# Splitting one group of products into 192 and 320 tokens, and issuing two row halves in order of time

## Chip, cores, metric

One core of a Trainium2 chip runs the kernel. The metric is the device time of one execution in microseconds (us); the time stated for a kernel is the median over its runs.

## The reference

The input x is 4 x 4096 x 192 (16384 tokens of 192 channels). A causal convolution of 7 taps with softmax weights per head goes ahead of two feed-forward blocks of 192 -> 2048 -> 192:

```python
x   = conv(x, softmax(weight))          # (16384, 192)
h1  = x @ moe_w_in                      # (16384, 2048)
x   = maximum(h1, 0) ** 2 @ moe_w_out   # (16384, 192)
h2  = x @ moe2_w_in
out = where(h2 > 0, h2, exp(minimum(h2, 0)) - 1) @ moe2_w_out
```

## The kernel before

The tokens go in 32 blocks of TB = 512. For each block and layer the 2048 hidden channels go in NP = 8 chunks of 256; one chunk of one block of one layer is a unit, and there are NU = 512 units. A planner (`merge` and `phases`) lists the units once; the main loop takes them in that order. In the round of unit u the kernel computes the first product h of unit u (`gemm1`), and the second product of unit u - 3 (`gemm2`, LAG = 3).

Every fp32 operand is kept as an upper part and a lower part in the type fp32r, and a product is the sum of three: upper by upper, upper by lower, lower by upper. After `gemm1`, ScalarE and VectorE make g from h, and split it into `gh` and `gl` (lines 740 and 745). `gemm2` multiplies g with the weights `wo`: its part A makes output channels 0 to 127 in the PSUM tile yA, with six products for a unit (four with `gh`, two with `gl`), its part B the last 64 channels in yB, with four products of which two are with `gl` (mostly 96 weight columns wide). `gemm1` makes two tiles h[0] and h[1] of 128 hidden channels, with nine products for each and row half, as listed below.

The contraction is cut across the TensorE's rows: each product is issued as two, one with rows 0 to 63 and one with rows 64 to 127. They are called half 0 and half 1, and each has its own list. All of them are 64 rows, 128 (or 96) weight columns and 512 tokens, and each loads its own weights (LDWEIGHTS, engine PEld in the profile). `products` (line 519 issues them) walks both lists in four turns, given by TURNS:

- turn 0: half 0 does part A (6), half 1 does part B (4)
- turn 1: half 0 does its work for h[0] (6), half 1 for h[1] (6)
- turn 2: half 0 does part B (4), half 1 does part A (6)
- turn 3: half 0 does h[1] (3), half 1 does h[0] (3)

So each half has 19 products in a unit. Before the change they are issued in pairs by `zip`: product k of half 0, then product k of half 1. So that the halves never add to the same PSUM tile at once, some products wait for the end of the other half's work on that tile: a `nop` on SyncE (line 524) waits for the product with index 5, 11 or 15 of half 1, and product 10 of half 1, 16 of half 0 or 0 of half 0 (of the next unit) waits for that nop. The same SyncE queue also issues most of the DMAs.

This form runs for u >= HALVES = 16 while both products exist, that is in rounds 16 to 511, 496 of them. Rounds 0 to 15 and the last three use lines 532 and 538: line 532 issues products over all 128 rows, and line 538 pairs of 64 rows for the first product's B rows. The convolution of the first blocks is done on TensorE in plain fp32 (line 400).

Of the kernel before, what the change touches and what calls it, by code (L numbers as in the profile page):

```python
# [19 lines left out]
TB = 512  # L20
# [45 lines left out]
def conv_moe_moe_kernel(  # L66
# [17 lines left out]
    nc = tc.nc  # L84
    B, S, D = x.shape
# [5 lines left out]
    DB = D - P  # L91
# [74 lines left out]
    def w_tiles(layer):  # L166
        if layer not in WS:
            tag = "w" if layer == 2 else "w1"
            WS[layer] = {
                s: cpool.tile([P, *dims], F32R, tag=f"{tag}{s}", name=f"w{s}{layer}") for s, dims in W_PARTS.items()  # L170
            }
        return WS[layer]
# [308 lines left out]
    def gemm2(layer, j, i, gh, gl):  # L481

        if i == 0:
            Y[layer, j] = [ps_y.tile([P, TB], F32, tag="y", name=f"y{layer}{s}") for s in "AB"]
        o = w_tiles(layer)["o"]
        hi, lo, b, bl = slice(0, P), slice(D + DB, 2 * D), slice(P, D + DB), slice(P, D + DB // 2)
        todo = {
            "A": [(s, d, g) for s in range(2) for d, g in ((hi, gh), (lo, gh))] + [(s, hi, gl) for s in range(2)],
            "B": [(s, b, gh) for s in range(2)] + [(0, bl, gl), (1, bl if i < NP - 1 else b, gl)],
        }  # L490
        work = {}
        for half in range(2):
            for y, part in zip(Y[layer, j], "AB"):
                begins = i == 0 and half == "AB".index(part)
                ends = i == NP - 1 and half != "AB".index(part)
                last = len(todo[part]) - 1
                work[half, part] = [
                    (o[:, 2 * i + s, d], g[:, s, :], y[0 : d.stop - d.start], begins and k == 0, ends and k == last)
                    for k, (s, d, g) in enumerate(todo[part])
                ]  # L500
        return work

# [1 line left out]


    TURNS = (("A", 0, "B", 1), ("B", 1, "A", 0))
    SIGNALS, WAITS = (5, 11, 15), {(10, 1): 5, (16, 0): 11, (0, 0): 15}
    SYNC = mybir.DependencyInfo(mybir.DependencyClass.Sync, mybir.DependencyReason.DATA)
    signals = {}

    def products(first, second, halves):

        if first and second and halves:
            work = {**first, **second}
            todo = [[w for what in TURNS[half] for w in work[half, what]] for half in range(2)]
            for k, pair in enumerate(zip(*todo)):
                for half, (w, x, o, st, sp) in enumerate(pair):
                    p = slice(half * DB, (half + 1) * DB)
                    m = nc.tensor.matmul(o, w[p], x[p], start=st, stop=sp)  # L519
                    after = signals.pop(WAITS.get((k, half)), None)  # L520
                    if after:
                        tc.add_manual_dep(m.ins, after.ins.name, SYNC, reason="the other half's products")
                    if half and k in SIGNALS:
                        signals[k] = nc.sync.nop()  # L524
                        tc.add_manual_dep(signals[k].ins, m.ins.name, SYNC, reason="the halves' products")
            return
        for do, parts in ((first, (0, 1)), (second, ("A", "B"))):
            for part in parts if do else ():
                order = (0, 1) if part in (0, "A") else (1, 0)
                begins, ends = (do[half, part] for half in order)  # L530
                for (w, x, o, st, _), (_, _, _, _, sp) in zip(begins, ends):
                    nc.tensor.matmul(o, w, x, start=st, stop=sp and part in ("A", "B"))  # L532
            if do is first and first:
                for k in range(3, 6):
                    for half in range(2):
                        w, x, o, _, _ = first[half, half][k]
                        p = slice(half * DB, (half + 1) * DB)
                        nc.tensor.matmul(o, w[p], x[p], start=False, stop=k == 5)  # L538
# [162 lines left out]
    with tc.manual_schedule():  # L701
# [61 lines left out]
        for u in range(NU + LAG):  # L763
# [12 lines left out]
            if 0 <= v:  # L776
                second = gemm2(*units[v], *gsplit.pop(v))
            products(u < NU and first, 0 <= v and second, u >= HALVES)
            for _ in range(3 if u < FIRST * NP else 2):
                if transfers and transfers[0][0] <= u:  # L780
# [65 lines left out]
```

## Time and profile before

| | |
|---|---|
| median of the runs | 2318.26 us (2318.13 to 2318.39) |
| the profiled execution's own time | 2319.63 us |
| its span, first to last instruction | 2317.9 us |
| granted TensorE clock, mean | 0.998 |
| busy: PE, PEld, DVE, ACT, POOL | 99%, 93%, 71%, 68%, 3% |
| matmul instructions, weight loads | 19282 each |

PE is TensorE's matmuls, PEld its weight loads, DVE VectorE, ACT ScalarE, POOL GpSimd, SPq the queue of SyncE. A matmul's record lasts longer than the distance to the next one, since matmuls are pipelined and their ends modelled; what one costs is read from the distance between the starts of two neighbours of the same half. The busy shares are averages over the span.

### The profile page before, as it was taken

The numbers are of one execution on the slowest core, as the hardware profiler recorded it, in microseconds if no ns is written. First come the engines' busy times: TensorE is split into PE (matmuls) and PEld (weight loads), VectorE is DVE, ScalarE is ACT, GpSimd is POOL, SyncE is SP. The second block draws the span as 40 slices with busy tenths as digits, with TensorE's granted clock in tenths as the row PEclk, the third lists the DMA queues.
The fourth block names the chain that finished last, engine by engine and source line by source line (L and its number), as shares of the span: only waits on it lengthen the run. The fifth ranks groups of instructions, "written<-read, shape, count | busy, mean of one in ns | idle before, by whom it ended". The sixth has DMA issues, their size and how long they took to land.

```text
span 2317.9 us, 46408 instructions
## 1 busy us (share of the span) xinstructions
PE 2305.2 (99%) x19282; PEld 2161.3 (93%) x19282; DVE 1652.1 (71%) x1968; ACT 1570.1 (68%) x1726; POOL 64.6 (3%) x81
## 2 busy tenths in 40 slices
PE   8999999999999999999999999999999999999999
PEld 5788998899999999999999999999999999999998
DVE  7768676777777776777767777777777676666665
ACT  7788888666666666666666666666666666777776
POOL 0012221000000000000000000000000000000000
PEclk9999999999999999999999999999999999999999
DMA  5112111111111111111111111111111110111111
GB/s 143 28 44 47 43 47 28 31 31 28 31 19 33 33 29 31 22 28 35 30 29 31 20 33 33 28 31 20 30 35 31 26 26 19 33 22 28 31 22 19
DMA packets 236721, 75.88 MB, mean 33 GB/s; under 512 B 208608, under 2 KB 220384, under 8 KB 236512
## 3 DMA queue, kind: packets, MB, share of 16 engines
q1 hardware_dynamic: 235440, 72.79, 14.2%
q8 instruction: 152, 2.49, 0.5%
q14 instruction: 57, 0.47, 0.1%
q10 hardware_dynamic: 1072, 0.13, 0.0%
HBM read 41.94 MB, written 25.17 MB: 29 GB/s over the span
## 4 chain that ended last, share of the span: by engine, by line
PE 97%; ACT 1%; DVE 1%; issue 0%; POOL 0%; SPq 0%; DVEq 0%; POOLq 0%; ACTq 0%
PE h L519 44%; PE y2A L519 15%; PE y1A L519 15%; PE y2B L519 10%; PE y1B L519 9%; PE h L532 1%; PE y1A L532 1%; PE h L538 1%; PE conv L400 1%; PE y1B L532 0%; ACT r L542 0%; ACT r L551 0%; PE warm L389 0%; PE y2A L532 0%; ACT gh L740 0%
## 5 line engine op out<-in xcount | busy, mean ns | idle before, releaser
L745 DVE TENSOR_TENSOR gl<-r,gh 128x1024 fp32r<-128x1024 f32 x512 | 633.7, 1238 | 410.4 <-ACT gh L740 410.4
L740 ACT CAST gh<-r 128x1024 fp32r<-128x1024 f32 x512 | 537.6, 1050 | 502.0 <-DVE r L555 292.3
L542 ACT ACTIVATE r<-h 128x1024 f32<-128x1024 f32 x512 | 525.1, 1026 | 193.7 <-PE h L519 184.4
L519 PE MATMUL y2A<-gh,wo 64*128 64x512 f32 x2024 | 554.1, 393 | 0.0
L519 PE MATMUL y1A<-gh,wo 64*128 64x512 f32 x1944 | 530.4, 392 | 0.7 <-SPq L524 0.6
L555 DVE SCALAR_TENSOR_TENSOR r<-r,h 128x1024 f32<-128x1024 f32 x256 | 312.7, 1222 | 205.7 <-ACT r L546 205.1
L519 PEld LDWEIGHTS y2A<-gh,wo 64*128 64x128 f32 x2024 | 356.2, 185 | 2.4
L519 PEld LDWEIGHTS y1A<-gh,wo 64*128 64x128 f32 x1944 | 345.2, 184 | 9.2 <-SPq L524 1.9
L519 PE MATMUL h<-x2Al,wAh 64*128 64x512 f32 x1024 | 323.5, 393 | 0.0
L519 PE MATMUL h<-x2Ah,wAl 64*128 64x512 f32 x1024 | 321.8, 391 | 0.0
L519 PE MATMUL h<-x2Ah,wAh 64*128 64x512 f32 x1024 | 321.4, 391 | 0.0
L519 PE MATMUL y2A<-gl,wo 64*128 64x512 f32 x1012 | 318.9, 395 | 0.0
L519 PE MATMUL y2B<-gh,wo 64*128 64x512 f32 x1012 | 316.3, 392 | 0.0
L519 PE MATMUL y2B<-gl,wo 64*96 64x512 f32 x1012 | 316.0, 392 | 0.0
L519 PE MATMUL y1A<-gl,wo 64*128 64x512 f32 x972 | 303.2, 391 | 0.0
L519 PE MATMUL y1B<-gh,wo 64*128 64x512 f32 x972 | 303.2, 391 | 0.0
L519 PE MATMUL y1B<-gl,wo 64*96 64x512 f32 x972 | 302.1, 390 | 0.0
L519 PE MATMUL h<-x1Ah,wAh 64*128 64x512 f32 x960 | 301.2, 393 | 0.0
L519 PE MATMUL h<-x1Ah,wAl 64*128 64x512 f32 x960 | 299.8, 391 | 0.0
L519 PE MATMUL h<-x1Al,wAh 64*128 64x512 f32 x960 | 299.6, 391 | 0.0
L546 ACT ACTIVATE r<-r 128x1024 f32<-128x1024 f32 x256 | 271.5, 1061 | 8.1
L553 DVE SCALAR_TENSOR_TENSOR r<-h,r 128x1024 f32<-128x1024 f32 x176 | 215.3, 1223 | 25.0 <-ACT r L542 22.9
(158 smaller groups left out, 4685.3 us busy)
## 6 DMA issues: line engine op xcount, KB each, us to landing
kept<-ya SPq DMA_DIRECT2D x32, 256.0 KB, 2.4
la<-kept SPq DMA_DIRECT2D x32, 256.0 KB, 3.1
lb<-kept SPq DMA_DIRECT2D x64, 128.0 KB, 3.0
out_dram<-zA SPq DMA_DIRECT2D x128, 64.0 KB, 2.0
xinA<-in_x_dram SPq DMA_DIRECT2D x126, 64.0 KB, 2.3
xinB<-in_x_dram SPq DMA_DIRECT2D x128, 32.0 KB, 1.9
kept<-ys SPq DMA_DIRECT2D x32, 128.0 KB, 2.4
out_dram<-zB SPq DMA_DIRECT2D x64, 64.0 KB, 2.0
```

What stands on the lines that cost most here:

```text
L400: nc.tensor.matmul(st[i], diag(i, k), t[:, k : k + n], start=k == 0, stop=k == K - 1)
L519: m = nc.tensor.matmul(o, w[p], x[p], start=st, stop=sp)
L532: nc.tensor.matmul(o, w, x, start=st, stop=sp and part in ("A", "B"))
L538: nc.tensor.matmul(o, w[p], x[p], start=False, stop=k == 5)
L542: nc.scalar.activation(out=r, in_=h, func=AF.Relu, scale=1.0 if layer == 1 else -1.0)
L546: nc.scalar.activation(out=r, in_=r, func=AF.Exp, scale=-1.0)
L553: nc.vector.scalar_tensor_tensor(out=r, in0=h, scalar=0.0, in1=r, op0=ALU.max, op1=ALU.mult)
L555: nc.vector.scalar_tensor_tensor(out=r, in0=r, scalar=-1.0, in1=h, op0=ALU.add, op1=ALU.max)
L740: nc.scalar.copy(out=gh, in_=gs[u])
L745: nc.vector.tensor_tensor(out=gl, in0=gs.pop(u), in1=f32(gsplit[u][0]), op=ALU.subtract)
```

## The change

In `gemm2`, each of part A's products with `gl` becomes two: one over tokens 0 to 191 and one over tokens 192 to 511, with the same weights and the same columns of yA. Each half has two such products in a unit, so its list grows from 19 products to 21. In `products`, the pairs of `zip` give way to a choice by time: each half has a clock that grows by the tokens of a product plus LOAD = 48, and the half whose clock is behind (half 0 at a tie) issues next. The nops and waits are placed by turns in place of indices: after both halves' last product of turns 0, 1 and 2 comes a nop, and the first product of turn 2, turn 3 and the next unit's turn 0 waits for it.

```diff
@@ -483,6 +483,7 @@
         o = w_tiles(layer)["o"]
+        WHOLE, CUT = (slice(0, TB),), (slice(0, D), slice(D, TB))
         hi, lo, b, bl = slice(0, P), slice(D + DB, 2 * D), slice(P, D + DB), slice(P, D + DB // 2)
@@ -495,8 +496,9 @@
                 work[half, part] = [
-                    (o[:, 2 * i + s, d], g[:, s, :], y[0 : d.stop - d.start], begins and k == 0, ends and k == last)
+                    (o[:, 2 * i + s, d], g[:, s, t], y[0 : d.stop - d.start, t], begins and k == 0, ends and k == last and t.stop == TB)
                     for k, (s, d, g) in enumerate(todo[part])
+                    for t in (CUT if g is gl and part == "A" else WHOLE)
                 ]
@@ -504,7 +506,7 @@
     TURNS = (("A", 0, "B", 1), ("B", 1, "A", 0))
-    SIGNALS, WAITS = (5, 11, 15), {(10, 1): 5, (16, 0): 11, (0, 0): 15}
+    LOAD = 48
@@ -512,17 +514,24 @@
             work = {**first, **second}
-            todo = [[w for what in TURNS[half] for w in work[half, what]] for half in range(2)]
-            for k, pair in enumerate(zip(*todo)):
-                for half, (w, x, o, st, sp) in enumerate(pair):
-                    p = slice(half * DB, (half + 1) * DB)
-                    m = nc.tensor.matmul(o, w[p], x[p], start=st, stop=sp)
-                    after = signals.pop(WAITS.get((k, half)), None)
+            todo = [deque((n, w) for n, what in enumerate(TURNS[half]) for w in work[half, what]) for half in range(2)]
+            clock, begun, last = [0, 0], set(), {}
+            while todo[0] or todo[1]:
+                half = 0 if todo[0] and (not todo[1] or clock[0] <= clock[1]) else 1
+                n, (w, x, o, st, sp) = todo[half].popleft()
+                p = slice(half * DB, (half + 1) * DB)
+                m = nc.tensor.matmul(o, w[p], x[p], start=st, stop=sp)
+                clock[half] += x.shape[-1] + LOAD
+                if n not in begun:
+                    begun.add(n)
+                    after = signals.pop((n + 2) % 4, None) if n != 1 else None
                     if after:
                         tc.add_manual_dep(m.ins, after.ins.name, SYNC, reason="the other half's products")
-                    if half and k in SIGNALS:
-                        signals[k] = nc.sync.nop()
-                        tc.add_manual_dep(signals[k].ins, m.ins.name, SYNC, reason="the halves' products")
+                last[n, half] = m
+                if n < 3 and (n, 1 - half) in last and all(not t or t[0][0] > n for t in todo):
+                    signals[n] = nc.sync.nop()
+                    for k in range(2):
+                        tc.add_manual_dep(signals[n].ins, last[n, k].ins.name, SYNC, reason="the halves' products")
             return
```

## Rows read from the trace of the kernel before

**Rows 1.** The page's part 1: busy time of each engine, share, instructions.

```profile
PE 2305.2 (99%) x19282; PEld 2161.3 (93%) x19282; DVE 1652.1 (71%) x1968; ACT 1570.1 (68%) x1726; POOL 64.6 (3%) x81
```

**Rows 2.** The page's part 4: the chain that ended last, by engine.

```profile
PE 97%; ACT 1%; DVE 1%; issue 0%; POOL 0%; SPq 0%; DVEq 0%; POOLq 0%; ACTq 0%
```

**Rows 3.** Busy time by stretch (instructions in brackets), granted clock, DMA share, GB/s.

```profile
105.30:2303.90 2198.60, 2197.89 (x18843) 2088.83 (x18843) 1563.37 (x1805) 1486.10 (x1597) 60.92 (x66) 1.00 0.14 30
```

**Rows 4.** Groups of instructions by form, PE: count, busy us, mean ns.

```profile
L519 PE MATMUL y2A<-gl,wo 64*128 64x512 f32 x1012 | 318.9, 395 | 0.0
...
L519 PE MATMUL y1A<-gl,wo 64*128 64x512 f32 x972 | 303.2, 391 | 0.0
```

**Rows 5.** Timeline, PE: the same turn of two units; start us, length us.

```profile
1201.57 0.58 PE L519 MATMUL h<-x2Ah,wAh 64*128 64x512 f32 x2
...
1206.01 0.59 PE L519 MATMUL h<-x1Ah,wAh 64*128 64x512 f32 x2
```

**Rows 6.** Timeline, part of turn 2: matmuls and weight loads, half 0 y2B, half 1 y2A.

```profile
1202.97 0.39 PE L519 MATMUL y2A<-gh,wo 64*128 64x512 f32 x1
1202.97 0.18 PEld L519 LDWEIGHTS y2A<-gh,wo 64*128 64x128 f32 x1
1203.16 0.40 PE L519 MATMUL y2B<-gh,wo 64*128 64x512 f32 x1
1203.17 0.18 PEld L519 LDWEIGHTS y2B<-gh,wo 64*128 64x128 f32 x1
1203.21 0.40 PE L519 MATMUL y2A<-gh,wo 64*128 64x512 f32 x1
1203.21 0.18 PEld L519 LDWEIGHTS y2A<-gh,wo 64*128 64x128 f32 x1
...
1203.40 0.39 PE L519 MATMUL y2B<-gh,wo 64*128 64x512 f32 x1
...
1203.67 0.39 PE L519 MATMUL y2A<-gh,wo 64*128 64x512 f32 x1
```

**Rows 7.** One line's instructions, L519 weight loads: min/median/max ns.

```profile
L519 PEld LDWEIGHTS y2B<-gh,wo x1012: 183/185/188, 402.9 to 2303.0; 64*128 64x128 f32 x169
...
L519 PEld LDWEIGHTS y2B<-gl,wo x1012: 157/158/188, 403.3 to 2303.4; 64*96 64x96 f32 x169
```

**Rows 8.** One line's instructions, L538: first product after the full-row products, and second.

```profile
L538 PE MATMUL h<-x1Bh,wBh x32: 493/498/792, 21.4 to 101.9; 64*128 64x512 f32 x32
...
L538 PE MATMUL h<-x1Bh,wBl x32: 388/389/628, 21.7 to 102.2; 64*128 64x512 f32 x32
```

**Rows 9.** Timeline of that place: L532's last product, then L538's pairs.

```profile
82.28 0.40 PE L532 MATMUL h<-x1Al,wAh 128*128 128x512 f32 x1
82.61 0.19 PEld L538 LDWEIGHTS h<-x1Bh,wBh 64*128 64x128 f32 x2 [0.37 <-issue]
82.61 0.51 PE L538 MATMUL h<-x1Bh,wBh 64*128 64x512 f32 x2
...
82.71 0.19 PEld L538 LDWEIGHTS h<-x1Bh,wBl 64*128 64x128 f32 x2
82.94 0.40 PE L538 MATMUL h<-x1Bh,wBl 64*128 64x512 f32 x2
```

**Rows 10.** One line's instructions, L400, the fp32 convolution: two matmuls a tap.

```profile
L400 PE MATMUL conv<-xtB,x2Bl x12: 378/378/379, 11.4 to 25.2; 128*128 128x256 f32 x12
...
L400 PE MATMUL conv<-xtA,x2Al x12: 591/592/697, 16.1 to 36.0; 128*128 128x512 f32 x12
```

**Rows 11.** Timeline, PE: five of the convolution's matmuls of 256 tokens.

```profile
24.11 1.24 PE L400 MATMUL conv<-xtB,x2Bl 128*128 128x256 f32 x5
```

**Rows 12.** Timeline, PE, L532's products over all 128 rows.

```profile
79.72 0.62 PE L532 MATMUL y1A<-gl,wo 128*128 128x512 f32 x2
80.18 0.39 PE L532 MATMUL y1B<-gh,wo 128*128 128x512 f32 x1
```

**Rows 13.** Waits: who waited for whom, us in total, times, longest.

```profile
ACT r L542 <- PE h L519: 184.4, 208, 3.9
...
PEld y1A L519 <- SPq L524: 1.9, 3, 1.1
```

## The prediction

> **What bounds the kernel now.** I read the busy times first [rows 1], then the chain that ended last [rows 2], then the stretch in which line 519 issues [rows 3]. The reader is to see that TensorE's matmuls are busy for 99% of the span, that 97% of the chain is PE, and that in the 2198.6 us from 105.3 to 2303.9 PE is idle for 0.7 us, with the granted clock at 1.00, its upper level of 2.4 GHz. ScalarE waits for PE's h 208 times, 184.4 us in all [rows 13], so it is ahead of PE, and a longer TensorE list lengthens the kernel one for one while a shorter one would shorten it.
>
> Then I read the timeline. The same turn of two neighbouring units starts 4.44 us apart [rows 5]. A half has 19 products in a unit, so one costs 4.44 / 19 = 233.7 ns. The turn in [rows 6] says the same: four products of half 1 start at 1202.97, 1203.21, (one not shown,) 1203.67, that is 0.70 / 3 = 233 ns, and half 0's go in the gaps between them. I take 233.5 ns. The records are 0.39 us long and overlap, so they are not the cost. At one column a cycle 512 columns are 512 / 2.4 = 213.3 ns; 20.2 ns of each product are something else, and the change hangs on what.
>
> **Part 1: the cut.** The 1012 and 972 products of yA with gl [rows 4] make 1984, which is 4 for each of 496 units, 2 for each half. Each becomes a piece of 192 and one of 320 columns. The columns stay the same (80 + 133.3 = 213.3 ns); a second product's fixed cost and a second weight load come on top. No line-519 product of the trace has fewer than 512 columns, so I bound the piece from both sides.
>
> First, the 20.2 ns as a fixed cost of any product: 192 columns take 80 + 20.2 = 100.2 ns, 320 take 153.5 ns. Second, as a slower flow of columns: the convolution's matmuls have records 214 ns longer for 256 more columns (592 against 378) [rows 10], and those of 256 columns start (1.24 - 0.38) / 4 = 0.215 us apart [rows 11], so hardly 2 ns are fixed there. If that holds for fp32r, the other 231.5 ns grow with the columns: 192 take 88.8 ns and 320 take 146.7 ns.
>
> Third, the weights. A load of 128 columns is recorded at 185 ns and one of 96 at 158 [rows 7]: 27 ns for 32 columns, so some 108 ns of the 185 pass with the columns and the rest is delay. Line 538's first product, which can't have its weights early, agrees: its record is 498 ns against 389 for the second [rows 8], 109 ns of waiting, and the second load starts 0.10 us after the first, before the first load's record ends [rows 9]. A half's next load starts when its running product starts (1203.21 and 1203.21 in [rows 6]). So no piece can give way to the next product in less than about 110 ns. That is nothing for 512 or 320 columns, and it raises the 192 piece from 89 or 100 to 110 ns.
>
> The pair of pieces is then 110 + 153.5 = 263.5 ns on the fixed reading and 110 + 146.7 = 256.7 on the other, against 233.5 for the whole product: 30.0 or 23.2 ns more. Neither reading is favoured by a row of fp32r, so I take the middle, 26.6 ns. A half has two such pairs in a unit, the other half has its own two in another turn, and the unit ends when both lists are done, so the unit grows by 2 x 26.6 = 53 ns, and 496 units by 26.4 us.
>
> The lower end is 2 ns for an extra product (the convolution's), if the load costs nothing: 2 x 2 x 496 = 2 us. The upper end, where the whole 185 ns of a load stand between two starts, is a rival below.
>
> The Trainium skill speaks here: TensorE: Matmul & The Clock Gate, Back-to-back issue gap, gives N / 2.4 + 2.5 ns for a warm product; by it the pieces would be 82.5 + 135.8 ns, 2.5 ns over the whole, and the change would cost 2.5 us. The spacing of 233.5 ns in [rows 6] is 17.7 ns above what the same formula gives for 512 columns, so it doesn't describe these products.
>
> **Part 2: the order.** It adds no instruction. By the code's clocks (560 for a whole product, 240 and 368 for the pieces) half 0 ends turn 0 at 3456 and half 1 at 2240; after turn 1 half 0 is 96 columns late against half 1's grid, 40 ns; in turn 2 half 1 has the pieces, and both end the unit at 10736. TensorE begins products in program order, so an order that differs from the true times would hold one half back. The true times differ from the clock's by 10 ns at most (110 against 240 / 2.4 = 100), and no place needs a load to pass more than one waiting product of the other half, as it does now: in [rows 6] half 1's load starts at 1203.21, ahead of half 0's product at 1203.40. I count nothing, and up to 2 us for jitter at ties. If that cover is gone it is the third rival.
>
> **Part 3: nops and waits.** Three nops a unit as before, at the same place of SyncE's queue among its DMAs, since all are issued inside one call. By the clocks the waiting product starts 2144, 2240 and 1680 columns after the end it waits for, against 2240, 2240 and 1680 before: only the first room shrinks, by 40 of 933 ns. The waits now cost 1.9 us in three events of the whole run [rows 13]. Behind the waiting instruction both halves' lists are queued, for TensorE's queue is one; ScalarE's line 542 would be the next to wait. I count nothing.
>
> **The sum.** Profiled execution 2319.63 + 26.4 = 2346.0 us; the median of the runs is 1.4 us below that execution, so 2344.7, and with a little jitter 2345 us, 1.2% slower. No change can be told here from a difference within 2%, 46 us, so the forecast counts as the same.
>
> **The rivals.**
>
> The cut is all but free: an extra product costs 2 ns, and the load hides. Result 2320 us. For it: [rows 10, 11]. Against it: the 109 ns of [rows 8] are longer than the 80 to 89 ns of a 192 piece.
>
> Small products run as the convolution's do: two matmuls of two cycles a column. By [rows 11] 256 columns cost 2 x 215 ns, so 192 cost some 2 x 162 = 323, 213 more than 110. Then 2 x 213 x 496 = 211 us more: 2556 us. It decides if the fp32r rate depends on the number of columns. No row shows fp32r at another size, for or against.
>
> The whole record of a load counts: a product can't start before 185 + 2 ns after the one before it on its half. Each piece then takes 187 ns, a pair 374, and 2 x 140.5 x 496 = 139 us come on: 2457 us. Against it: [rows 9], where the next load already starts after 0.10 us.
>
> Loads are no longer ahead of the products: in the new order two pieces of one half sometimes stand one behind the other. If a load is exposed for each extra product, 2 x 109 x 496 = 108 us come on: 2426 us, 4.7% slower; it decides as soon as a load starts later than its own half's running product. The Trainium skill, TensorE: Matmul & The Clock Gate, section The mechanism, lets a load run beside a running matmul only on other rows; by it the loads of both pieces would always be exposed. [Rows 6] contradict it: half 1's load and half 1's product start together and run side by side.
>
> A nop is late: the order puts it at another moment against SyncE's DMAs, and TensorE waits. A tenth of a us a unit would be 50 us: 2395 us. Against it: 1.9 us of such waits now [rows 13].
>
> Faster: the 20.2 ns come from both halves starting at once, and the new order spreads them. If 17 whole products of each half lost them, 17 x 20.2 x 496 = 170 us would go: about 2175 us. Against it: the halves are 40 and 190 ns apart already [rows 6], and products over all 128 rows, with no second half, stand 0.23 us apart too [rows 12].
>
> **How the numbers follow.** My forecast 0.70; all but free 0.08; small products slow 0.07; loads no longer ahead 0.05; whole load records 0.04; a late nop 0.04; faster 0.02. The first two and a part of the late nop lie within 2%: 0.79. Slower by over 2%: 0.19. Faster: 0.02. The range takes in the free cut at its lower end and, at its upper end, both readings with a few ns more a piece and small late waits: 2320 to 2376, which leaves out about 2 in 10.
>
> **What would show it.** In the changed kernel's profile there should be some 21266 matmuls, groups of 64x192 and of 64x320, 1012 and 972 of each by layer, and PE busy at 99% still. From the start of a 192 piece to the 320 piece of the same half I expect 0.11 us, from there to the next product of that half 0.15, between whole products 0.23, and the same turn of two units 4.49 us apart. Spacings of 0.19 after both pieces mean the load's whole record; 0.3 after the 192 piece, or two records for it, mean the slow rate; a load that starts well after its half's running product means the order; more waits for line 524's successor mean the nops. I am wrong if a whole product's spacing moves from 0.23 in either direction, since I took it as given.

## The result and the profile after

The changed kernel takes 2342.95 us (median of 2 runs, 2341.6 to 2344.3) against 2318.26: 24.7 us more, a ratio of 1.0107 with a 95% interval from 1.0063 to 1.015. It is slower, by an amount within the 2% that count as the same here. The forecast was 2345.

The page's part 1 and the chain by engine answer to [rows 1, 2]:

```profile
PE 2327.9 (99%) x21298; PEld 2167.0 (93%) x21298; DVE 1654.2 (71%) x1968; ACT 1573.9 (67%) x1726; POOL 64.7 (3%) x81
...
PE 98%; ACT 1%; DVE 1%; issue 0%; POOL 0%; SPq 0%; DVEq 0%; ACTq 0%; POOLq 0%
```

TensorE has 2016 matmuls more: the 1984 of the forecast, and 32 from the cut products in the rounds outside the new order, which the forecast left out (2 for each of 16 units). It is as busy as before, and the other engines' busy times are the same. The stretch in which line 523 issues, by engine, answers to [rows 3]:

```profile
105.30:2325.90 2220.60, 2220.07 (x20810) 2092.12 (x20808) 1564.35 (x1804) 1489.06 (x1596) 60.95 (x66) 1.00 0.14 30
```

PE is idle for 0.5 us of it, and the clock is granted in full. So the 22 us more of this stretch are TensorE's own time. The pieces, from the groups by form (count, busy us, mean ns):

```profile
L523 PE MATMUL y2A<-gl,wo 64*128 64x320 f32 x1012 | 297.4, 329 | 0.0
...
L523 PE MATMUL y2A<-gl,wo 64*128 64x192 f32 x1012 | 251.2, 248 | 0.0
```

Each piece has one record, so no piece is split again. What it costs is in the timeline of a turn 2, matmuls and weight loads; half 1 does yA, and half 0, whose rows are left out, does yB. The last two rows are the first products of turn 3 in this unit and in the next, 4.49 us apart, as forecast:

```profile
1200.47 0.40 PE L523 MATMUL y2A<-gh,wo 64*128 64x512 f32 x1
...
1200.70 0.25 PE L523 MATMUL y2A<-gl,wo 64*128 64x192 f32 x1
1200.70 0.19 PEld L523 LDWEIGHTS y2A<-gl,wo 64*128 64x128 f32 x1
...
1200.79 0.33 PE L523 MATMUL y2A<-gl,wo 64*128 64x320 f32 x1
1200.82 0.19 PEld L523 LDWEIGHTS y2A<-gl,wo 64*128 64x128 f32 x1
...
1200.96 0.42 PE L523 MATMUL y2A<-gl,wo 64*128 64x192 f32 x2
...
1201.22 0.58 PE L523 MATMUL h<-x2Ah,wAh 64*128 64x512 f32 x2
...
1205.71 0.58 PE L523 MATMUL h<-x2Ah,wAh 64*128 64x512 f32 x2
```

From the start of a whole product to the next it is 0.23 us, as in [rows 6]. A pair of pieces takes 0.26 (1200.70 to 1200.96, and to 1201.22), the 192 piece 0.09 of it and the 320 piece 0.17. The reader is to look at the loads: the load for the 320 piece starts with the 192 piece at 1200.70, and the next load only at 1200.82, 0.12 later (the median over the trace is 108 ns) and 0.03 after the 320 piece's record began. A record can begin before its weights are there; the wait then lies inside it, as in [rows 8].

The waits for SyncE's nop and for h, which answer to [rows 13]:

```profile
ACT r L551 <- PE h L523: 197.3, 203, 4.0
...
PEld y1A L523 <- SPq L532: 1.8, 3, 0.9
```

### The profile page after: what moved, and what is told of

Its sections match the earlier page's. It is cut to its first block, busy times and chain, and to the rows that moved or that the text cites. A ratio compares the mean times of both kernels' runs of the same rounds, so it can differ in the third digit from the quotient of the medians.

```text
span 2339.9 us, 50440 instructions
## 1 busy us (share of the span) xinstructions
PE 2327.9 (99%) x21298; PEld 2167.0 (93%) x21298; DVE 1654.2 (71%) x1968; ACT 1573.9 (67%) x1726; POOL 64.7 (3%) x81
## 4 chain that ended last, share of the span: by engine, by line
PE 98%; ACT 1%; DVE 1%; issue 0%; POOL 0%; SPq 0%; DVEq 0%; ACTq 0%; POOLq 0%
PE h L523 41%; PE y2A L523 19%; PE y1A L523 17%; PE y1B L523 9%; PE y2B L523 8%; PE h L541 1%; PE y1A L541 1%; PE h L547 1%; PE conv L400 1%; PE y1B L541 0%; ACT r L551 0%; ACT r L560 0%; PE warm L389 0%; PE y2A L541 0%; PE y2B L541 0%
## 5 line engine op out<-in xcount | busy, mean ns | idle before, releaser
L523 PEld LDWEIGHTS y1A<-gh,wo 64*128 64x128 f32 x1944 | 358.3, 185 | 26.6 <-SPq L532 1.8
L523 PE MATMUL h<-x2Al,wAh 64*128 64x512 f32 x1024 | 344.6, 392 | 0.0
L523 PE MATMUL h<-x2Ah,wAh 64*128 64x512 f32 x1024 | 344.2, 391 | 0.0
L523 PE MATMUL h<-x2Ah,wAl 64*128 64x512 f32 x1024 | 344.1, 391 | 0.0
L523 PE MATMUL y2A<-gl,wo 64*128 64x192 f32 x2024 | 342.5, 289 | 0.0
L523 PEld LDWEIGHTS y2A<-gl,wo 64*128 64x128 f32 x2024 | 318.1, 186 | 16.1
L523 PE MATMUL y1A<-gl,wo 64*128 64x192 f32 (+1 forms) x1944 | 329.3, 289 | 0.0
L523 PE MATMUL h<-x1Ah,wAl 64*128 64x512 f32 x960 | 324.1, 390 | 0.0
L523 PE MATMUL h<-x1Al,wAh 64*128 64x512 f32 x960 | 323.6, 391 | 0.0
L523 PE MATMUL h<-x1Ah,wAh 64*128 64x512 f32 x960 | 323.0, 390 | 0.0
L523 PEld LDWEIGHTS y1A<-gl,wo 64*128 64x128 f32 x1944 | 305.7, 185 | 14.7
```

## The experiments

The theory with which they began (A): at 512 columns fp32r flows at 0.452 ns a column with about 2 ns fixed for a product, and a piece that flows for less than about 110 ns makes whatever follows on its half wait for its weights. Its rival (B): the 20 ns above 512 / 2.4 are fixed for each product. A third (C): a cut costs what it costs, wherever it lies. Every difference below is against the kernel before in the same set of runs; divided by the 2 x 496 = 992 cut pairs of a half it gives the cost of a pair.

**Order alone.** The cut is taken out of the changed kernel.

```diff
-                    for t in (CUT if g is gl and part == "A" else WHOLE)
+                    for t in WHOLE
```

> The products stay whole; only the choice by clock and the placing of nops by turns remain. Theory (the whole cost is the cut's): the clocks are equal at every step, the order is the old one, 2318 us. Rival (the nops and waits cost part of it): between 2320 and 2343 us.

Measured: 2317.2 us against 2318.09, ratio 0.9999 (0.999 to 1.0008). The new placing of the nops costs nothing by itself. The order by time is not tested here, since with whole products it is the old order; the cut in the old order, below, tests it.

**The cut at 256.**

```diff
-        WHOLE, CUT = (slice(0, TB),), (slice(0, D), slice(D, TB))
+        WHOLE, CUT = (slice(0, TB),), (slice(0, 256), slice(256, TB))
```

> The cut is at 256 in place of 192. No piece is shorter than the 109 ns that a load takes to become usable. Theory A (the load binds the short piece, and apart from that columns flow at one rate with some 2 ns fixed for a product): a pair costs 2 to 4 ns over a whole product, 2320 to 2322 us. Theory B (each product has some 20 ns fixed, whatever its size): a pair costs 20 ns more, 2338 us. Theory C (a cut costs the same 26 ns wherever it lies): 2343 us.

Measured: 2317.01 us, ratio 0.9994 (0.9986 to 1.0003). The same number of extra products, and no cost. B and C fall. Theory A's 2 to 4 ns a pair are not there either: the interval ends 0.7 us above the kernel before, which is 0.7 ns a pair. The timeline of a turn 2 (matmuls only):

```profile
1200.58 0.28 PE L523 MATMUL y2A<-gl,wo 64*128 64x256 f32 x1
...
1200.70 0.40 PE L523 MATMUL y2A<-gl,wo 64*128 64x256 f32 x2
...
1200.94 0.28 PE L523 MATMUL y2A<-gl,wo 64*128 64x256 f32 x1
...
1201.06 0.46 PE L523 MATMUL h<-x2Ah,wAh 64*128 64x512 f32 x2
```

Each piece takes 0.12 us, a pair 0.24: to the accuracy of the rows a whole product's 0.23.

**The cut at 128.** The same line, with 128 in place of 256.

> The cut is at 128. Theory A (load binds, columns at one rate): 109 ns for the short piece and 384 columns at 0.452 ns + 2 = 176 ns, 285 ns a pair, 52 over a whole product, 1984 / 2 x 52 = 51 us: 2369 us. Theory B with the binding load: 109 + 180 = 289 ns, 2373 us; theory B without it: 2338 us. Theory C: 2343 us.

Measured: 2366.51 us against 2318.09, ratio 1.0208 (1.0194 to 1.0222): 48.4 us, 49 ns a pair against 52 by theory A. Two pairs of one turn, each row a 128 piece with the 384 piece behind it:

```profile
1200.74 0.45 PE L523 MATMUL y1A<-gl,wo 64*128 64x128 f32 x2
...
1201.04 0.45 PE L523 MATMUL y1A<-gl,wo 64*128 64x128 f32 x2
```

0.30 us a pair. The smaller the short piece, the dearer the cut.

**Narrower weights.** Part B's products with gl, most of which load 96 weight columns, are cut at 192 in place of part A's.

```diff
-                    for t in (CUT if g is gl and part == "A" else WHOLE)
+                    for t in (CUT if g is gl and part == "B" else WHOLE)
```

> Part B's products with the lower part of g are cut at 192 in place of part A's; they load 96 weight columns in place of 128 (seven of eight chunks all four, the last chunk two of four). Theory A: the load is usable after some 109 - 27 = 82 ns and hides under 89 ns, so only the last chunk's two pay: 2320 to 2323 us. Theory B: 20 ns a pair, 2338 us. Theory C: 2343 us.

Measured: 2323.2 us, ratio 1.0023 (1.0014 to 1.0032): 5.1 us where the same cut of part A costs 24.7. That is the upper end of theory A's 2320 to 2323. By it one pair in eight of a half waits some 20 ns, 62 x 20 ns = 1.2 us in all; the other 3.9 us are some 4 ns a pair, which that wait does not explain. The timeline of a turn 2, the cut half's products and loads:

```profile
1202.72 0.25 PE L523 MATMUL y2B<-gl,wo 64*96 64x192 f32 x1
1202.72 0.16 PEld L523 LDWEIGHTS y2B<-gl,wo 64*96 64x96 f32 x1
...
1202.81 0.40 PE L523 MATMUL y2B<-gl,wo 64*96 64x320 f32 x2
1202.81 0.31 PEld L523 LDWEIGHTS y2B<-gl,wo 64*96 64x96 f32 x2
...
1203.05 0.31 PE L523 MATMUL y2B<-gl,wo 64*96 64x320 f32 x1
```

The load behind the 192 piece starts 0.09 us after the one before it (1202.81), with its product, where it was 0.12 with 128 columns; from one 320 piece to the next (a whole pair) it is 0.24, not 0.26.

**Narrower weights, cut at 128.** As the last, with the cut at 128. Its rival is that two products of a half must stand some 110 ns apart whatever their weights.

> Part B's products with the lower part of g (96 weight columns, but for two of four in the last chunk) cut at 128 in place of 192; part A whole. Theory A: the load's wait grows with its weight columns, so the next weights are there some 112 - 27 = 85 ns after a piece's start; the 128 piece flows for 60 ns, 25 short, so a pair costs 25 + 2 to 5 ns: 27 to 30 us, 2344 to 2347 us, and the spacing behind the 128 piece is 25 ns above 176. Rival (what binds is a fixed distance of 110 ns between two products of a half): 128 pieces cost as in part A, 50 us, 2366 us.

Measured: 2345.6 us against 2318.04, ratio 1.0118 (1.0104 to 1.0132): 27.6 us, 28 ns a pair, inside theory A's 27 to 30. Matmuls of half 1 in a turn 0:

```profile
1203.36 0.42 PE L523 MATMUL y2B<-gl,wo 64*96 64x128 f32 x2
...
1203.63 0.22 PE L523 MATMUL y2B<-gl,wo 64*96 64x128 f32 x1
...
1203.69 0.36 PE L523 MATMUL y2B<-gl,wo 64*96 64x384 f32 x1
```

A pair takes 0.27 us, against 0.30 with 128 weight columns. The load binds, and it does so by its columns: behind a 128 piece the next load starts 82 ns after the one before it (median over the trace), where it is 108 with 128 weight columns.

**The cut at 224.**

```diff
-        WHOLE, CUT = (slice(0, TB),), (slice(0, D), slice(D, TB))
+        WHOLE, CUT = (slice(0, TB),), (slice(0, 224), slice(224, TB))
```

> The cut is at 224. Theory A: the short piece flows for 224 x 0.452 + 2 = 103 ns, 6 short of 109, so a pair costs 6 ns more than with the cut at 256, which cost nothing measurable: 6 x 992 = 6 us, 2323 us, with a spread from 2320 to 2326. Rival (the cost is a step between 192 and 256, not a shortfall against the load): 2317 or 2343 us.

Measured: 2328.28 us against 2316.96, ratio 1.0051 (1.0038 to 1.0064): 11.3 us, 11 ns a pair. It is a slope and not a step, but above theory A's 6 ns. The time from load to load is not what is above it. Loads at the end of a group of pieces, first with the cut at 128, then at 224; the first row of each two is the longer piece's load, which starts with the short piece, and the second the next load of that half:

```profile
1201.04 0.18 PEld L523 LDWEIGHTS y1A<-gl,wo 64*128 64x128 f32 x1
1201.15 0.19 PEld L523 LDWEIGHTS h<-x2Ah,wAh 64*128 64x128 f32 x1
...
1200.77 0.18 PEld L523 LDWEIGHTS y2A<-gl,wo 64*128 64x128 f32 x1
1200.88 0.21 PEld L523 LDWEIGHTS h<-x2Ah,wAh 64*128 64x128 f32 x2
```

They stand 0.11 us apart in both; over the 992 groups of pieces of each trace the median is 108 ns with cuts at 128, 192 and 224 alike, the least 107 and the most 113. The rest lies in the longer piece behind the short one: from its load to the next the median is 179, 151 and 137 ns, where 0.452 ns a column + 2 gives 176, 147 and 132. Why it takes 3 to 5 ns more there was not tried. At 128 these two distances make a pair of 287 ns, and the run shows 282; that difference is open too.

**The long piece first.**

```diff
-        WHOLE, CUT = (slice(0, TB),), (slice(0, D), slice(D, TB))
+        WHOLE, CUT = (slice(0, TB),), (slice(0, 320), slice(320, TB))
```

> The pieces change places: tokens 0 to 319, then 320 to 511. Theory A (whatever follows a 192 piece waits some 20 ns for its weights): the 320 piece takes 147 ns, the 192 piece 88, and the product behind it (the second 320 piece, or the first whole product of the next turn) 20 ns more than its own; 2343 us. Rival (the second piece on the same tile pays): the 192 piece would take some 110 ns, the rest its usual.

Measured: 2339.45 us against 2316.96, ratio 1.01 (1.0086 to 1.0114): 22.5 us, the same cost within the intervals. Matmuls of half 0 in a turn 0 and the two products behind it:

```profile
1200.61 0.31 PE L523 MATMUL y2A<-gl,wo 64*128 64x320 f32 x1
...
1200.76 0.42 PE L523 MATMUL y2A<-gl,wo 64*128 64x192 f32 x2
...
1201.02 0.25 PE L523 MATMUL y2A<-gl,wo 64*128 64x192 f32 x1
1201.11 0.42 PE L523 MATMUL h<-x2Ah,wAh 64*128 64x512 f32 x1
...
1201.37 0.40 PE L523 MATMUL h<-x2Ah,wAl 64*128 64x512 f32 x1
```

The first 320 piece takes 0.15 us, as its columns do, since a whole product went ahead of it; the 192 piece and the 320 piece behind it take 0.26 together (1200.76 to 1201.02). And the first whole product of the next turn takes 0.26 in place of 0.23 (1201.11 to 1201.37) though nothing in it was cut: it follows a 192 piece. Its record is 0.42 us long, 0.03 more than its like.

**The cut in the old order.** The kernel before with the cut, and the indices of nops and waits moved to the ends of the longer turns.

```diff
+        WHOLE, CUT = (slice(0, TB),), (slice(0, D), slice(D, TB))
...
-                    (o[:, 2 * i + s, d], g[:, s, :], y[0 : d.stop - d.start], begins and k == 0, ends and k == last)
+                    (o[:, 2 * i + s, d], g[:, s, t], y[0 : d.stop - d.start, t], begins and k == 0, ends and k == last and t.stop == TB)
                     for k, (s, d, g) in enumerate(todo[part])
+                    for t in (CUT if g is gl and part == "A" else WHOLE)
...
-    SIGNALS, WAITS = (5, 11, 15), {(10, 1): 5, (16, 0): 11, (0, 0): 15}
+    SIGNALS, WAITS = (7, 13, 17), {(10, 1): 7, (18, 0): 13, (0, 0): 17}
```

> The cut at 192 with the old order: product k of half 0, then product k of half 1, 21 each; nops and waits moved to the ends of the longer turns (7, 13, 17). Theory (products begin in program order, so the half without pieces holds back the half with them): starts laid out by hand with 109, 147 and 233.5 ns give 4.67 us a unit, 240 ns more than before, 2436 us. Rival (the halves run independently of the order): 2343 us as with the order by time.

Measured: 2340.9 us against 2316.96, ratio 1.0109 (1.0093 to 1.0124). My theory of the order fell: it costs the same as by time. The timeline of a turn 0 shows why (half 0 does yA and then h, half 1 is already in h):

```profile
1200.96 0.39 PE L521 MATMUL h<-x2Ah,wAh 64*128 64x512 f32 x1
1201.06 0.42 PE L521 MATMUL y2A<-gl,wo 64*128 64x192 f32 x2
1201.19 0.39 PE L521 MATMUL h<-x2Ah,wAl 64*128 64x512 f32 x1
1201.32 0.42 PE L521 MATMUL y2A<-gl,wo 64*128 64x192 f32 x2
1201.42 0.39 PE L521 MATMUL h<-x2Al,wAh 64*128 64x512 f32 x1
1201.57 0.39 PE L521 MATMUL h<-x2Ah,wAh 64*128 64x512 f32 x1
1201.65 0.40 PE L521 MATMUL h<-x2Bh,wBh 64*128 64x512 f32 x1
```

In the list of pairs, half 0's first 192 piece (index 4) stands ahead of half 1's product 4, yet that one begins at 1200.96 and the piece at 1201.06. Four pieces later half 0 begins its product 8 at 1201.57, ahead of half 1's product 7 at 1201.65, which stands ahead of it in the list. Each half keeps its own pace: 0.23 between half 1's products, 0.26 for half 0's pairs.

**Six cuts in place of two.** All of part A's products are cut at 256, so that a half has six extra products in a unit. Only the first piece of the first product on a tile carries the mark (`start`) that begins its sum.

```diff
-        WHOLE, CUT = (slice(0, TB),), (slice(0, D), slice(D, TB))
+        WHOLE, CUT = (slice(0, TB),), (slice(0, 256), slice(256, TB))
...
-                    (o[:, 2 * i + s, d], g[:, s, t], y[0 : d.stop - d.start, t], begins and k == 0, ends and k == last and t.stop == TB)
+                    (o[:, 2 * i + s, d], g[:, s, t], y[0 : d.stop - d.start, t], begins and k == 0 and t.start == 0, ends and k == last and t.stop == TB)
                     for k, (s, d, g) in enumerate(todo[part])
-                    for t in (CUT if g is gl and part == "A" else WHOLE)
+                    for t in (CUT if part == "A" else WHOLE)
```

> All six of part A's products of each half are cut at 256, six extra products a half and unit in place of two, 5952 in all. Theory A (a product over 256 columns costs nothing but its columns and a few ns): between 2317 us (nothing) and 2330 us (4.5 ns each, the difference of 119 + 119 to 233.4 seen with two cuts). Theory B (20 ns fixed): 2377 us.

Measured: 2326.56 us against 2318.04, ratio 1.0033 (1.0021 to 1.0045): 8.5 us for 6 x 496 = 2976 extra products of a half, 2.9 ns each (1.6 to 3.5 by the interval). Theory B's 20 ns are not there. As a fixed part of every product the 2.9 ns are not settled: the two cuts at 256 above cost at most 0.7 ns a pair, and why the two runs differ is open. The 2.5 ns of the Trainium skill, TensorE: Matmul & The Clock Gate, Back-to-back issue gap, lie inside the interval of the six cuts and outside that of the two; the flow of 0.452 ns a column that goes with it here does not agree with that page's 1 / 2.4.

The same run answers a rival of theory A, that the loads of both halves wait for one another. It has 50 loads in a unit, 46 of 128 weight columns and mostly 4 of 96; one behind the other, at 108 and 82 ns, they would take 5.3 us, and 2326.56 us for 512 units leave no more than 4.54 us for one. So the loads of the two halves overlap, and the wait is a half's own.

No version beats the kernel before beyond its interval; the order alone and the cut at 256 are the same as it.

## Why the prediction was right, point by point

**The bound.** TensorE's list sets the time: PE idle for 0.5 of 2220.6 us after the change, and the other engines as busy as before. As predicted.

**The sum.** 26.6 ns a pair were forecast and 24.7 us / 992 = 24.9 ns were measured; 26.4 us against 24.7. Of the two readings whose middle I took, the fixed 20 ns are wrong (the cuts at 256) and the flow by columns is right; it alone gave 23.2 ns. So the middle was a compromise with a reading that had no share in it, and that it came within 2 ns was luck: the load's interval is 108 ns, close to the 110 that I took, and what lifts the pair above 23.2 ns is the 320 piece, 151 ns from its load to the next where 146.7 were counted, for a reason that no run shows.

**The binding load.** The bound from [rows 7 to 9] was right and is nearly the whole cost: it went with the size of the short piece (49, 25, 11 and no ns with cuts at 128, 192, 224 and 256), and with the weight columns (28 ns at 128, 5 at 192, for mostly 96 columns). Where it shows was wrong: I expected 0.11 us from the 192 piece to the 320 piece and 0.15 from there on, and the products' records start 0.09 and 0.17 apart. The 0.11 and 0.15 are there between the starts of the loads (108 and 151 ns): a matmul's record begins before its weights are there, and the wait lies in the record that follows the short piece.

**The order.** The step "TensorE begins products in program order, so an order that differs from the true times would hold one half back" failed. Nothing was counted for it, so the time was not touched; but the order by time is needed for nothing here, as the cut in the old order shows. The rows of the kernel before spoke against the step already: in [rows 6] half 0's product 12, its first of yB, begins at 1203.16, ahead of half 1's product 11 at 1203.21, which stands ahead of it in the list of pairs. A rule of the Trainium skill, TensorE: Matmul & The Clock Gate, section The mechanism, by which matmuls start in the order of the program, is contradicted by the rows of the cut in the old order. How far a half may run ahead stays open: I ran no kernel whose pieces ask for more than these.

**Nops and waits.** 1.8 us in three waits after, 1.9 in three before: nothing, as counted.

**The rivals.** The cut that is all but free is true at 256 and not at 192. Small products at the convolution's rate (a pair of pieces takes 0.26 us) and whole load records (0.19 between starts) do not occur. Nor do exposed loads: the load at 1200.70 starts with its half's 192 piece, and a pair costs 25 ns more and not 109. Spreading the halves gained nothing that can be seen: whole products still stand 0.23 us apart after the change. The order alone doesn't test this, since with whole products it spreads nothing.

## What to carry to other kernels

Before a product is cut, compare the flow of its shorter piece with the time from one weight load to the next (here 108 ns for 128 weight columns, 82 for 96). As long as the piece is longer, a cut here costs 0 to 4 ns; below that the product behind it pays the difference, whoever it is. Look for that wait inside the record of the follower and not in the gap ahead of it. An unseen size is best bounded from rows that show the parts separately (flow per column, load per weight column, fixed part), and a bound that decides a forecast deserves the row that separates two readings, not their middle.

## What the runs showed of the hardware

Behind a short piece a half's next weight load starts 108 ns after its last with 128 weight columns (107 to 113) and 82 ns with 96 (81 to 85), in these fp32r products at a granted clock of 1.00, though a load's record lasts 185 and 158 ns [rows 7]. Where a piece flows for less than that, the next product's record begins on time and holds the wait.

Two products on different halves of the rows don't keep the order of the list: in the cut in the old order half 0's product 8 began 0.08 us ahead of half 1's product 7.

At a granted clock of 1.00 these fp32r products flow at some 0.45 ns a column (0.12 us for 256 columns, 0.23 for 512), 7 to 8% slower than one column a cycle at 2.4 GHz (0.417). The fixed part of a product is at most a few ns: 2.9 with six cuts, none to be measured with two. What slows the flow was not tried; the fp32 convolution's 214 ns for 256 columns at two cycles each [rows 10] don't show it.
